# A transformer kernel's projections: products for maxima held back until their tiles have had a fixed while

## The chip, the cores and the metric

The kernel runs on one core of one Trainium2 chip. The metric is the time of one execution on the device in microseconds (us), as the median of several runs. A matrix product runs on TensorE (PE), with its weight loads listed apart (PEld); VectorE is DVE, ScalarE is ACT, GpSimd is POOL, and SyncE is SP, whose queue issues nearly all DMAs.

## The reference

Two layers, each an attention block and a feed-forward block, both with a layer norm ahead and a residual around. S = 2048 rows, D = 640, 32 heads of 20, F = 1536, all float32.

```python
x = A_x
x = x + _A_ref(_layernorm(x), A_wqkv, A_wo)
x = x + _B_ref(_layernorm(x), B_w1, B_b1, B_w2, B_b2)
x = x + _A_ref(_layernorm(x), A_wqkv, A_wo)
x = x + _B_ref(_layernorm(x), B_w1, B_b1, B_w2, B_b2)
```

_A_ref projects to q, k and v, forms scores q k^T / sqrt(20) for each head, takes the softmax over the 2048 keys, multiplies by v and projects back with wo. _B_ref is (relu(x w1 + b1))^2 w2 + b2.

## The kernel before, in words

Each layer has three stages: projections with a good part of the maxima (qkv, lines 728 to 997), attention (lines 1010 to 1222), and the output projection with the feed-forward block (add_heads and mlp). The first layer's projections fill the trace to about 310 us and the second layer's the stretch from 1757 to 2048 us.

Operands of the projections and of the scores are split into a high and a low part of a type that TensorE takes in one pass, and a product is the sum of three part products. The results q and k are therefore stored to DRAM in three parts (d_qk, and d_kd for differences of neighbouring key blocks) by SP, from a tile named ev that ScalarE and GpSimd fill, and read back into tiles of another layout (k, q, kd), in which one half of the partitions holds even heads and the other odd ones.

The softmax needs the maximum of each row of scores first. The kernel gets it by a pass of its own: products of queries by keys (by_queries, line 477), whose 512 results VectorE reduces to one number. There are two forms. A *single* (smax, line 488; "one" in the planner) is one product and one reduction (L492). A *double* (step_one and both_one, lines 535 and 543) takes two blocks of keys at once: one product with the difference of the two key blocks (tile kd), a Relu on ScalarE (L540), a second product with one of the blocks, and one sum-and-maximum on VectorE (L548). So a double spends half the VectorE time per product.

Heads go in groups g of four, queries in blocks qb of 512 rows (t = 4 g + qb), keys in blocks c of 512. A group of work in the planner is (g, qb, c), where c is 0 to 3 for singles and "d" or "e" for doubles (blocks 0 and 1, or 2 and 3). It has eight pairs (p, sub) of PAIRS, each done for par = 0 and 1.

The projection stage is written as one stream by a planner that runs while the program is built. Its units are pairs (tb, pos) of a row block and a column block (UNITS, line 724), followed by the products for v; each unit is 15 products for each half of the 128 partitions, and the two halves run side by side (product, line 310; L330 in the trace). The planner has a clock, now, that says how far it takes TensorE, VectorE and ScalarE to be: a step of two half products adds 0.235 us to now["pe"] (0.155 in the v part, line 962), a set of transposes 1.2 (line 865), and a product for maxima takes the place of one half product in a step. At each step insert() (line 854) asks whether the next bank of PSUM is free by that clock; if so, choose() (line 816) takes the next piece of work, otherwise, or if choose() gives None, the half product of the projections runs.

following() (line 796) hands out the pieces. When its queue is empty it takes the next group from its list (groups for singles, double for doubles), asks for that group's tiles with tiles() (line 771), which issues DMAs on SP only for tiles that aren't there, asks for the tiles of the next one or two groups of the list too, and fills the queue with the group's eight pairs.

Tiles are mostly asked for earlier than that, at fixed places of the stream (lines 972 to 988), by the lists PLAIN and DOUBLE (lines 705 to 718): the tiles of a single group are asked for two units before the group is entered in groups, those of the first double group two units before the doubles are entered. soon holds groups whose tiles were asked for. end_group() (line 782) gives up a q tile when no group in soon, in the lists or in the queues needs it; a tile needed later is then loaded again.

SP issues in order, and a store of ev waits there until GpSimd has filled the tile, with all requests behind it.

The projection stage ends with its last product. What is not done of the maxima by then goes to the list todo of attention (line 1024), in pairs: one entry is one (t, p, sub, c), with both halves of partitions. In attention an order written out by hand (ORDERS, line 1002) interleaves the scores, the exponentials, the products with v and the maxima of later blocks, for eight tiles of keys at a time. The number of pairs in it, 12 to 16, is chosen by pairs() (line 1183): 8 times the pairs that must be done by a block's start over the tiles left until then, collected as a debt, and at least 12. The order of 12 repeats one pattern of nine operations; the others are irregular. In the order of 12, a third of the pairs is done in halves of 256 keys (smax_half, L527). The exponentials are ScalarE's (L615, L617).

Of the kernel before, what the change touches and what calls it, by code (L numbers as in the profile page):

```python
# [39 lines left out]
def tile_layers(  # L40
# [26 lines left out]
    def slot(shape, dtype, label):  # L67
        return arena.tile(shape, dtype, tag="slot", name=name(label))
# [362 lines left out]
    def rows_of_heads(dst, src, g):  # L431
        src = src[4 * g * DH : (4 * g + 4) * DH]
        src = src.rearrange("(a b d) s t -> b (d s) a t", a=2, b=2)
        for par in range(2):
            dma(nc.sync, dst[64 * par : 64 * par + 3 * DH], src[par])

    def load_k(g, c, keep):

        if not keep:
            k = slot([P, 2, QB], F32R, "k")  # L440
        elif (g % 4, c) in kept:
            k = kept[g % 4, c]
        else:
            k = kept[g % 4, c] = slot([P, 2, QB], F32R, "k")
            for par in range(2):
                dma(nc.sync, k[64 * par + 60 : 64 * par + 62], d_one)
        k_t[g, c] = k
        rows_of_heads(k, d_qk[1, c], g)

    def load_q(t):  # L450
        g, qb = divmod(t, NQB)
        q_t[t] = slot([P, 2, QB], F32R, "q")
        rows_of_heads(q_t[t], d_qk[0, qb], g)

    def load_kd(g, x):
        k_t[g, x] = slot([P, 2, QB], F32R, "kd")
        rows_of_heads(k_t[g, x], d_kd["de".index(x)], g)
# [266 lines left out]
    UNITS = [(tb, pos) for tb in range(NQB) for pos in range(FIRST)]  # L724
    UNITS += [(tb, pos) for pos in range(FIRST, 10) for tb in range(NQB)]
    READY = 0.9

    def qkv(first, x_src, rest, scores):

# [5 lines left out]
        turning = []  # L735
        now = {"pe": 0.0, "dve": 0.0, "act": 0.0}
        busy = [0.0] * 8
        early, late, soon = {}, {}, []
        coming = [y for x in DOUBLE for h in x for y in h if y[2] == "d"]

        def at(when, n, f):
# [29 lines left out]
        def tiles(x):  # L771
            g, qb, c = x
            for c in [c] if c in range(4) else [c, 2 * "de".index(c)]:
                if (g, c) not in k_t:
                    if c in range(4):
                        load_k(g, c, g > 1)
                    else:
                        load_kd(g, c)
            if g * NQB + qb not in q_t:
                load_q(g * NQB + qb)  # L780

        def end_group(x):
            g, qb, c = x
            t = g * NQB + qb
            rest = soon + groups + double + [w[0] for w in work + twos] + [o["w"][0] for o in begun]
            if t == 0:
                left[t] -= 1 if c in range(4) else 2
            if (t or left[t]) and all(y[:2] != (g, qb) for y in rest):
                del q_t[t]
            use = {(y[0], y[2]) for y in rest + coming}  # L790
            use |= {(h, 2 * "de".index(y)) for h, y in use if y not in range(4)}
            for y in [y for y in k_t if y[0] == g and y not in use]:
                if g < 2 or y[1] not in range(4):
                    del k_t[y]

        def following(todo, queue):

            if not queue:
                if not todo:
                    return None  # L800
                x = todo.pop(0)
                tiles(x)
                for y in todo[: 2 if len(xt_) < NQB else 1]:
                    tiles(y)
                queue.extend((x, p, sub) for p, sub in PAIRS)
            return queue.pop(0)
# [9 lines left out]
        def choose():  # L816

            kind = state["last"]
            if kind == "one" or not (groups or work):
                if begun and begun[0]["ready"][0] < now["pe"] and len(begun[0]["r"]) == 2:  # L820
                    return begun.pop(0) | {"kind": "both"}
                if len(begun) < 2:
                    w = following(double, twos)
                    if w:
                        begun.append({"kind": "step", "w": w, "r": [], "ready": []})
                        return begun[-1]
            w = following(groups, work)
            return {"kind": "one", "w": w} if w else None
# [57 lines left out]
        def step_rest():  # L886
# [3 lines left out]
            if turn:  # L890
                turning.append((max(now["dve"] + READY, N * 0.235 - 0.1), turn))

# [60 lines left out]
        for j in range(len(chains)):  # L953
# [20 lines left out]
            if step % 2 == 0 and 0 <= b <= NQB:  # L974
                if b < NQB and PLAIN[b][step // 2]:
                    tiles(PLAIN[b][step // 2][0])
                    soon.append(PLAIN[b][step // 2][0])
                new = PLAIN[b][0] if step and b < NQB else PLAIN[b - 1][1] if not step and b else []
                groups.extend(new)
                soon[:] = [y for y in soon if y not in new]  # L980
                if step and b < NQB and DOUBLE[b][0]:
                    tiles(DOUBLE[b][0][0])
                    soon.append(DOUBLE[b][0][0])
# [393 lines left out]
    def layer(first, x_a, x_m, x_e, front_0, ahead):  # L1377
        xs = []
        scores = attention(first, x_a, xs)
        qkv(first, x_a, front_0, scores)  # L1380
        next(scores, None)
        steps = []
# [191 lines left out]
```

## Time and profile before

| what | value |
|---|---|
| median of 3 runs | 3500.96 us (3500.59 to 3501.50) |
| the profiled execution | 3503.38 us, its span 3501.0 us |
| PE, PEld busy | 3483.9 us (100%), 2184.4 us (62%) |
| DVE, ACT, POOL busy | 2726.4 us (78%), 2603.0 us (74%), 811.1 us (23%) |
| L492, singles' reduction | 2092, 686 ns on the mean |
| L527, reduction of two halves | 984, 682 ns |
| L548, doubles' reduction | 510, 689 ns |
| L540, doubles' Relu | 510, 597 ns |
| clock granted to TensorE, mean | 1.0 |

All times in views of the trace are microseconds from the start of the span. In a timeline, a row gives start and length, engine, line, operation, tiles and count; a bracket at its end is the time that the engine stood idle before it, with what it waited for. Matmuls overlap, and their ends are modelled, so a busy PE is not a PE at its peak; its gaps are the safer reading. In a row of the windows, the columns are the stretch, its length, then for each engine the busy time with the number of instructions in brackets, in the order PE, PEld, DVE, ACT, POOL, then the granted clock, the busy share of the DMA engines and GB/s. Where a row is for one source line alone, only its engine stands there.

### The profile page before, as it was taken

To read this page: it belongs to the slowest core of one execution; us is meant where nothing else is said; L and a number is where in the kernel's file an instruction comes from. 1 tells how busy PE (TensorE), PEld (TensorE's weight loads), DVE (VectorE), ACT (ScalarE), POOL (GpSimd) and SP (SyncE) were. 2 spreads that over 40 slices of the span, in tenths; PEclk is the share of its full clock that TensorE was granted. 3 is DMA by queue.
4 is the path that set the end of the run, shared out by engine and by line. 5 is a ranking of instruction groups with operands and counts; after the bars stand their busy time and mean duration, and the time that the engine had idled before them with its cause. 6 is when DMAs were issued, how large, how long until landed. Compare 5 with 4: busy or idle time off the path is not lost.

```text
span 3501.0 us, 69729 instructions
## 1 busy us (share of the span) xinstructions
PE 3483.9 (100%) x26544; PEld 2184.4 (62%) x26544; DVE 2726.4 (78%) x5023; ACT 2603.0 (74%) x4218; POOL 811.1 (23%) x927
## 2 busy tenths in 40 slices
PE   9999999999999999999999999999999999999999
PEld 7897444444444446999988964444444444479998
DVE  8878999999999993455567789999999999824443
ACT  3778999999999994222237789999999999932221
POOL 6530444221221121111153201211211221211110
PEclk9999999999999999999999999999999999999999
DMA  9766555323211136734477652232232111376221
GB/s 300 277 232 177 177 156 166 111 71 83 58 49 51 45 114 215 252 106 109 134 268 247 201 153 69 77 83 59 71 83 61 46 49 44 115 237 231 79 80 38
DMA packets 377404, 452.69 MB, mean 129 GB/s; under 512 B 176642, under 2 KB 223746, under 8 KB 377070
## 3 DMA queue, kind: packets, MB, share of 16 engines
q1 hardware_dynamic: 376254, 445.89, 42.1%
q8 instruction: 208, 3.41, 0.4%
q10 hardware_dynamic: 816, 2.36, 0.2%
q14 instruction: 126, 1.03, 0.1%
HBM read 273.83 MB, written 174.30 MB: 128 GB/s over the span
## 4 chain that ended last, share of the span: by engine, by line
PE 96%; DVE 1%; DMA 1%; issue 1%; ACT 0%; POOL 0%; SPq 0%; DVEq 0%
PE banks L621 29%; PE banks L480 20%; PE banks L607 14%; PE banks L292 13%; PE banks L1340 10%; PE banks L330 10%; DMA q<-d_qk 1%; PE banks L1172 0%; ACT e L1179 0%; DVE bst L243 0%; DVE mx L492 0%; SPq L76 0%; DVE xnT L256 0%; DVE x L251 0%; DMA d_qk<-ev 0%
## 5 line engine op out<-in xcount | busy, mean ns | idle before, releaser
L492 DVE TENSOR_REDUCE mx<-banks 128x1 f32<-128x512 f32 x2092 | 1427.0, 686 | 155.3 <-PE banks L480 51.3
L480 PE MATMUL banks<-k,q 60*128 60x256 f32 (+1 forms) x4570 | 1313.7, 369 | 3.5 <-DVE v L376 1.8
L480 PEld LDWEIGHTS banks<-k,q 60*128 60x128 f32 x4570 | 729.7, 184 | 880.0 <-DVE mx L527 814.3
L615 ACT ACTIVATE e<-banks 128x512 f32<-128x512 f32 x1988 | 1198.1, 608 | 23.3 <-PE banks L607 4.6
L607 PE MATMUL banks<-q,k 62*128 62x512 f32 x3968 | 1095.8, 424 | 0.7 <-DVE mx L548 0.7
L621 PE MATMUL banks<-e,vg 128*32 128x512 f32 x8192 | 1091.8, 605 | 1.5 <-ACT e L1179 1.5
L617 ACT ACTIVATE e<-banks 128x1024 f32<-128x1024 f32 x990 | 1015.3, 1026 | 0.3
L527 DVE TENSOR_REDUCE mx<-banks 128x2 f32<-128x512 f32 x984 | 671.3, 682 | 1.7 <-PE banks L480 1.7
L607 PEld LDWEIGHTS banks<-q,k 62*128 62x128 f32 x3968 | 584.3, 184 | 15.4 <-ACT e L615 6.8
L548 DVE CUSTOM_DVE_ANT_0 rl<-banks,rl 128x512 f32<-128x512 f32 x510 | 332.7, 689 | 101.2 <-PE banks L480 90.6
L330 PE MATMUL banks<-xnT,wqk 64*128 64x512 f32 x2400 | 378.5, 394 | 0.3 <-ACT mark_t L332 0.3
L1325 ACT ACTIVATE r<-banks,b_t 128x512 f32<-128x512 f32 x96 | 66.2, 690 | 419.8 <-PE banks L292 418.5
L540 ACT ACTIVATE rl<-banks 128x512 f32<-128x512 f32 x510 | 270.8, 597 | 99.3 <-PE banks L480 91.2
L1340 PE MATMUL banks<-w,h 128*128 128x320 f32 x2304 | 340.4, 309 | 0.0
L1340 PEld LDWEIGHTS banks<-w,h 128*128 128x128 f32 x2304 | 339.2, 188 | 1.3
L292 PE MATMUL banks<-xnT,w 128*128 128x512 f32 x1440 | 329.4, 389 | 0.0
L621 PEld LDWEIGHTS banks<-e,vg 128*32 128x32 f32 x8192 | 161.1, 108 | 261.8 <-issue 240.3
L330 PEld LDWEIGHTS banks<-xnT,wqk 64*128 64x128 f32 x2400 | 285.8, 185 | 34.6 <-issue 2.4
L292 PEld LDWEIGHTS banks<-xnT,w 128*128 128x128 f32 x1440 | 269.6, 188 | 55.3
L665 POOL TENSOR_TENSOR few<-few,minus_t 128x16 f32<-128x16 f32 x62 | 179.9, 2901 | 357.0 <-DMA few<-d_s 350.7
L270 POOL CAST mr<-nt 128x32 fp32r<-128x32 f32 x64 | 13.5, 211 | 943.0 <-DVE nt L574 915.0
L330 PE MATMUL banks<-wv,xnT 64*128 64x320 f32 x1920 | 199.1, 307 | 0.9 <-ACT mark_t L332 0.9
(90 smaller groups left out, 2280.7 us busy)
## 6 DMA issues: line engine op xcount, KB each, us to landing
q<-d_qk SPq DMA_DIRECT2D x242, 240.0 KB
d_qk<-ev SPq DMA_DIRECT2D x80, 512.0 KB
k<-d_qk SPq DMA_DIRECT2D x152, 240.0 KB
x<-d_x SPq DMA_DIRECT2D x84, 320.0 KB
d_qk<-ev SPq DMA_DIRECT2D x80, 256.0 KB
d_o<-ot SPq DMA_DIRECT2D x248, 80.0 KB
ot<-d_o SPq DMA_DIRECT2D x38, 512.0 KB
d_v<-v SPq DMA_DIRECT2D x32, 512.0 KB
```

Source lines behind the costliest of these rows:

```text
L292: nc.tensor.matmul(dst, a, b, start=(n == 0), stop=(n == last))
L330: m = nc.tensor.matmul(ch["dst"][:, :width], *pair, start=first, stop=last)
L480: return nc.tensor.matmul(dst, q_t[t][b : b + 60, p, sub * P : (sub + 1) * P], k_t[t // NQB, c][b : b + 60, p, keys], start=True, stop=True,)
L492: nc.vector.tensor_reduce(maxima(t)[:, 2 * par + p, sub, c : c + 1], dst, axis=AX.X, op=ALU.max)
L527: r = nc.vector.tensor_reduce(maxima(t)[:, p : p + 3 : 2, sub, c if not half else column(t, p, sub)], bank.rearrange("q (r k) -> q r k", r=2),
L540: nc.scalar.activation(res, dst, AF.Relu)
L548: nc.vector.tensor_tensor_reduce(out=r, in0=dst, in1=r, scale=1.0, scalar=LEAST, op0=ALU.add, op1=ALU.max, accum_out=maxima(t)[:, 2 * par ...
L607: nc.tensor.matmul(dst, k_t[t // NQB, kt // 4][b : b + 62, p, (kt % 4) * P : (kt % 4 + 1) * P], q_t[t][b : b + 62, p, :], start=True, stop ...
L615: nc.scalar.activation(es[h], dst, AF.Exp, scale=SCALE)
L617: nc.scalar.activation(es[pair], banks[:, 1:3, :], AF.Exp, scale=SCALE)
L621: nc.tensor.matmul(acc[32 * h : 32 * h + 32, :], v_t[t // NQB, kt // 8][:, kt % 8, 32 * h : 32 * h + 32], es[h], start=(kt == 0), stop=(kt ...
L1340: nc.tensor.matmul(dst[:, :HALF], hs[f][:, hx, i * P : (i + 1) * P], w_2.piece(at_2(f0 + f, hw, hf)), start=(f == 0 and (hx, hw) == THREE[0]),
```

## The change

following() used to take a group off its list and begin it at once. Now it asks for the group's tiles and leaves the group on the list until landed() is true: until the planner's clock for TensorE stands at least 10.7 us (singles) or 11.7 us (doubles) past the moment at which the group's key tile and its q tile were asked for, whichever was later. Until then following() returns None. In choose() a double that is held lets a single through; if there is none either, insert() returns False and the projections go on. tiles() writes down when each tile was asked for. The request for the tiles of the groups after it stays behind the start of the group, and so comes after the hold. No instruction is added, and none waits for anything new.

```diff
--- before.py
+++ after.py
@@ -724,6 +724,7 @@
     UNITS = [(tb, pos) for tb in range(NQB) for pos in range(FIRST)]
     UNITS += [(tb, pos) for pos in range(FIRST, 10) for tb in range(NQB)]
     READY = 0.9
+    LANDS = {False: 10.7, True: 11.7}
 
     def qkv(first, x_src, rest, scores):
 
@@ -735,7 +736,7 @@
         turning = []
         now = {"pe": 0.0, "dve": 0.0, "act": 0.0}
         busy = [0.0] * 8
-        early, late, soon = {}, {}, []
+        early, late, soon, asked = {}, {}, [], {}
         coming = [y for x in DOUBLE for h in x for y in h if y[2] == "d"]
 
         def at(when, n, f):
@@ -772,12 +773,19 @@
             g, qb, c = x
             for c in [c] if c in range(4) else [c, 2 * "de".index(c)]:
                 if (g, c) not in k_t:
+                    asked[g, c] = now["pe"]
                     if c in range(4):
                         load_k(g, c, g > 1)
                     else:
                         load_kd(g, c)
             if g * NQB + qb not in q_t:
+                asked[g, qb, "q"] = now["pe"]
                 load_q(g * NQB + qb)
+
+        def landed(x):
+            g, qb, c = x
+            late = c not in range(4)
+            return now["pe"] >= max(asked.get(y, -99) for y in ((g, c), (g, qb, "q"))) + LANDS[late]
 
         def end_group(x):
             g, qb, c = x
@@ -798,8 +806,11 @@
             if not queue:
                 if not todo:
                     return None
-                x = todo.pop(0)
+                x = todo[0]
                 tiles(x)
+                if not landed(x):
+                    return None
+                todo.pop(0)
                 for y in todo[: 2 if len(xt_) < NQB else 1]:
                     tiles(y)
                 queue.extend((x, p, sub) for p, sub in PAIRS)
```

## The prediction

> **What bounds the kernel now.** I read the page first, for the time and the chain of waits; then the PE timeline of the two projection stages for every gap; then the SP timeline for the requests that end in those gaps; then the busy times by stage.
>
> ```profile
> span 3501.0 us, 69729 instructions
> ...
> PE 96%; DVE 1%; DMA 1%; issue 1%; ACT 0%; POOL 0%; SPq 0%; DVEq 0%
> ```
>
> The chain that ends last is TensorE almost throughout; transfers hold 1% of it. The change touches only the two projection stages, so the question is what TensorE loses there. Gaps stand in brackets in the PE timeline: one in the first layer, four in the second.
>
> ```profile
> 74.97 0.62 PE L330 MATMUL banks<-xnT,wqk 64*128 64x512 f32 x3
> 76.72 0.47 PE L480 MATMUL banks<-kd,q 60*128 60x512 f32 x1 [1.13 <-DMA q<-d_qk]
> ...
> 1785.10 0.47 PE L480 MATMUL banks<-k,q 60*128 60x512 f32 x1 [0.31 <-DMA q<-d_qk]
> 1785.76 0.70 PE L480 MATMUL banks<-k,q 60*128 60x512 f32 x3 [0.18 <-DMA q<-d_qk]
> ...
> 1795.98 0.46 PE L480 MATMUL banks<-k,q 60*128 60x512 f32 x1 [1.18 <-DVE mx L474]
> ...
> 1816.52 0.47 PE L480 MATMUL banks<-kd,q 60*128 60x512 f32 x1 [1.83 <-DMA q<-d_qk]
> ```
>
> Each is the first product of a group: (0,1,d) at 76.72 and 1816.52, (0,0,0) at 1785.10 and 1785.76 (its two halves of rows), (1,0,0) at 1795.98. The last is put down to a memset of VectorE (L474); no product reads that, and the request of q (1,0) had gone out 5 us before, so I count it as a transfer too. Sum: 1.13 + 0.31 + 0.18 + 1.18 + 1.83 = 4.63 us.
>
> ```profile
> 69.50 7.08 DMA q<-d_qk
> ...
> 1779.54 0.85 SPq L76 DMA_DIRECT2D q<-d_qk  x2
> ...
> 1790.96 0.82 SPq L76 DMA_DIRECT2D q<-d_qk  x2
> ...
> 1799.22 0.95 SPq L76 DMA_DIRECT2D q<-d_qk  x2
> ...
> 1805.33 0.99 SPq L76 DMA_DIRECT2D kd<-d_kd  x2
> ...
> 1807.33 9.06 DMA q<-d_qk
> ...
> 1778.00:1785.00 7.00, 6.80 (x60) 5.27 (x58) 0.00 (x0) 2.44 (x8) 3.67 (x3) 1.00 0.97 305
> ...
> 1796.00:1816.00 20.00, 18.69 (x156) 17.84 (x156) 18.42 (x30) 4.58 (x12) 6.41 (x6) 1.00 1.02 324
> 1816.00:1850.00 34.00, 33.48 (x280) 27.94 (x282) 27.98 (x71) 19.09 (x41) 17.90 (x19) 1.00 0.98 348
> 1850.00:1900.00 50.00, 50.00 (x422) 40.36 (x420) 39.34 (x124) 38.47 (x80) 19.07 (x20) 1.00 0.63 225
> ```
>
> The first rows are requests and landings of q (SP timeline and chain), the last four the stages of the second layer (PE, PEld, DVE, ACT, POOL, clock, DMA share, GB/s). While the gaps occur the 16 DMA engines are full (0.97 to 1.02), and q takes 7 to 9 us from issue to landing; from 1850 on there is room (0.63) and TensorE has no gap.
>
> **The change part by part.** It adds no instruction. It reorders TensorE's stream: a group's products stay out until the planner's clock stands 10.7 (11.7 for d and e) past the request, and projection matmuls run in their place, as insert() returns False.
>
> Which groups are held follows from the planner's arithmetic. Requests go out two units ahead: 2 x 15 steps x 0.235 = 7.05, plus 1.2 for each set of transposes between, plus 0.1175 for each product inserted. For (0,0,0) that is 10.65 in the first layer (three sets) and 7.05 in the second. In the second layer (1,0,0) follows with 7.05 + 16 x 0.1175 = 8.93, then (0,0,1) with 9.63 and (0,1,d) with 9.40; in the first layer (0,1,d) has 8.93, and the others have 11.5 or more. Later groups are requested when the group ahead begins, so they have the length of a group.
>
> ```profile
> 30.00:308.00 278.00, 164.37 (x501) 1.00 0.78 260
> ...
> 1785.61 9.71 DVE mx L492 x16
> ```
>
> The first row counts L548: two records each, so 250 reductions of doubles between 76.7 and 308, 0.93 us apart, 16 in a group: 14.8 us, more than 11.7 (by the planner's clock at the least 11.87). So these aren't held, or by a step. The second row is the first single group: 16 reductions in 9.71 us by the trace, 8.93 by the planner.
>
> Held are then: first layer, (0,0,0) by one step and (0,1,d) by 11.7 - 8.93 = 2.77 us; second layer, (0,0,0) by 3.65 and (0,1,d) by 1 to 2.3. (1,0,0) now starts at the end of the delayed (0,0,0), 12.6 after its request, and (0,0,1) about 13.5 after its own.
>
> *Stalls.* At (0,0,0), 3.65 later than 1785.1 is past both landings: 0.49 gone. (1,0,0) comes at about 1757.5 (first projection matmul of the layer) + 40.85 = 1798.3, past 1795.98: 1.18 gone. First layer, (0,1,d): 2.77 exceeds 1.13, and the five or so single products that run in between have their tiles: 1.13 gone.
>
> (0,1,d) in the second layer is the tight one. Nine products fewer lie before its request, which comes at 45.2 instead of 46.1; it is released at 56.9, on the trace 1814.4. Its q landed at 1807.33 + 9.06 = 1816.4, on full engines, so an earlier request alone doesn't bring it sooner. But (0,0,0) now ends (40.85) after line 977 has entered (0,0,1) in soon, so end_group keeps q (0,0), which before was deleted and loaded again at 1799.22.
>
> ```profile
> q<-d_qk SPq DMA_DIRECT2D x242, 240.0 KB
> ```
>
> That takes 2 x 240 KB off the queue, at 324 to 348 GB/s 1.4 us: landing about 1814.9, left over 0.5 us. Bounds: 0, when the landing moves along with the 2.6 us by which TensorE is earlier, and 2.0, when the reload gives nothing. I take 0.5, as it comes from the rate of the very window. The Trainium skill (DMA: Bandwidth & Descriptors, Specifications) gives a fabric ceiling of 435 GB/s; the fullest window here shows 348. By the page's figure the remaining queue would be gone before 1814.4, an estimate that makes the left-over zero; the measured rate decides.
>
> *Moved requests.* following() asks for the next group's tiles only after the hold: for (1,1,d), four issues of SP, 1.3 to 2.8 us later than before, past a few stores of ev. Their products begin 23 us after that; nothing.
>
> *Products that slip.* What isn't done in the projections is done in attention. Second layer: 3.65 us without singles is 6.5 products; 1.3 come back as the pause of 0.7 us before (0,0,1) goes, and about one as singles and doubles then run together. Some 4.2 are missing when doubles begin, 5.5 at the end, since projections are two steps further on: 1.4 sets of a double's four products. First layer: about 1.9 products, 0.4 sets. In the projections each is worth 50.00 / 422 = 0.118 us of TensorE (row of 1850): 7.4 x 0.118 = 0.87 us saved.
>
> In attention each set comes back as two of the pairs in todo.
>
> ```profile
> 308.00:1352.00 1044.00, 675.00 (x984) 1.00 0.36 102
> ...
> 308.00:1352.00 1044.00, 335.65 (x492) 1.00 0.36 102
> ...
> 2047.00:3092.00 1045.00, 672.34 (x980) 1.00 0.27 74
> ...
> 2047.00:3092.00 1045.00, 335.67 (x492) 1.00 0.27 74
> ...
> 517.84 1.00 PE banks L621 x8
> ...
> 519.85 1.00 PE banks L621 x8
> ...
> 1317.08 1.00 PE banks L621 x8
> ...
> 1319.09 0.99 PE banks L621 x8
> ...
> 900.00:932.60 32.60, 32.60 (x259) 14.53 (x257) 30.52 (x51) 32.33 (x51) 6.62 (x7) 1.00 0.20 52
> ```
>
> Reductions L492 and L527 in attention, by layer: (984 + 492) / 2 = 738 pairs, and 736. pairs() divides by 496 - 3 - 1 = 492 tiles: 8 x 738 / 492 = 12.00. The first layer sits exactly on the smallest pace; the second has two pairs to spare. Each pair beyond makes one order of 12 an order of 13. The trace shows none. Below: with products (517.84) and without (1317.08) a tile of attention takes 2.01 us, as ScalarE is full (32.33 of 32.60), so a pair may cost nothing; a gain has no way in, as the count of activations stays. Above: two reductions end to end, 2 x 0.69 = 1.4 us. By VectorE's share, 30.52 of 32.60 a block or 15.26 of 16.3 an order, 26 / 24 of that is 16.5: 0.2 us. I take that, as it is the row of the same stage. Sets are whole: layer one slips 0 or 1, layer two 1 or 2, so 0 to 4 such orders; I take 2: 0.4 us.
>
> *Sum*, against the profiled execution of 3503.38 us (span 3501.0): -4.63 + 0.5 - 0.87 + 0.4 = -4.6, so 3498.8. That execution lies 2.42 above the median of 3500.96; on the median's level: 3496.4 us, 0.13% less. About 0.2%, 7 us, is what I treat as the least that a measurement of this kernel can tell from no change.
>
> **The rivals.** *The queue sets the pace (stalls stay).* TensorE reaches (0,1,d) and (1,0,0) earlier, stores of ev come earlier, and full engines (1.02) deliver no sooner; holds only trade places with stalls. For it: the share of DMA in 1778 to 1850. Against: the hold exceeds the stall at four of five gaps. It gives 0.49 + 0.87 - 0.4 = 1.0 less, and up to 2 with the first layer's gap: 3499.5. The Trainium skill (DMA: Bandwidth & Descriptors, Queues, rings and completion order) says that an engine consumes descriptors in ring order; by that rule a load waits for all stores asked before it, which is this rival; the landings of 7 to 9 us in the rows agree with it, though none shows the order itself.
>
> *The slipped maxima cost more than the stalls.* Place: attention, orders of 13, which leave the regular alternation of the order of 12. Price: up to 1.4 us each. If two sets slip in the first layer (4 pairs) and three in the second (6, two of them free), there are 8: 11.2 us, against 4.1 + 20 x 0.118 = 6.5 saved: 4.7 slower, 3505.7. It decides from four orders at 1.4 us, or 27 at 0.2. For it: 12.00 exactly, and VectorE at 94%. Against: ScalarE is the fuller, and my count is 0 to 4.
>
> *A larger gain.* If holds recur in later groups by steps and 25 products more slip into free attention, 4.1 + 32 x 0.118 = 7.9 less: 3493.1. Against: 14.8 us per group.
>
> *It does nothing.* The clock that counts is the planner's; if it ran ahead of TensorE holds would end too early. But the request at 1779.54 and the product at 1785.10 lie as the planner has them (7.05 apart from the first issue at 1778.05). It gives 3501.
>
> **How the numbers follow.** Forecast 0.60, queue 0.14, slipped maxima 0.14, larger gain 0.08, nothing 0.04. Only the larger gain passes 7 us downwards, and only the worst third of the slipped maxima, plus a point for what I don't see, upwards: faster 0.08, same 0.86, slower 0.06. Low: all stalls gone, twice the slip, orders free, -4.63 - 1.75 = -6.4, and part of the larger gain: 3493.0. High: past the queue's and the idle case to part of the slipped maxima: 3503.0.
>
> **What would show it.** Right: no bracketed gap at these five places; first layer-two product at about 1789; two q issues fewer in the second layer's projections; L492 plus L527 in attention up by 0 to 4 pairs a layer; attention's blocks at 32.6 us. Wrong: a gap above 1 us before a kd product; attention longer by more than 2 us; more than 6 pairs slipped in a layer.

## The result and the profile after

The changed kernel takes 3549.27 us (median, 3548.64 to 3551.31) beside 3500.78 for the kernel before: a ratio of 1.0141, 95% interval 1.0129 to 1.0153. The forecast was 3496.4 in a range of 3493.0 to 3503.0. It is wrong, in sign too. From the page of the profile after: its length, the chain by engine, and the loads of q.

```profile
span 3549.5 us, 69631 instructions
...
PE 95%; ACT 2%; DVE 1%; issue 1%; POOL 0%; DMA 0%; ACTq 0%; POOLq 0%; DVEq 0%
...
q<-d_qk SPq DMA_DIRECT2D x240, 240.0 KB
```

The share of transfers in the chain is gone, and two loads of q as well; but ScalarE, at 0% before, now holds 2%. The PE timeline after, at the groups that had waited (first (0,1,d) of the first layer; (0,0,0) and (0,1,d) of the second):

```profile
77.75 0.39 PE L480 MATMUL banks<-kd,q 60*128 60x512 f32 x1
...
1809.16 0.63 PE L480 MATMUL banks<-k,q 60*128 60x512 f32 x4
...
1834.95 0.39 PE L480 MATMUL banks<-kd,q 60*128 60x512 f32 x1
```

No bracket is left at any of the five places, and no gap over 0.2 us has come up at another product for maxima while the projections run. So the holds do what they say. Where the time went shows when the two traces are cut into stages. First the chain: where the first layer's attention ends (L292, before and after), where the second layer's projections begin (L330), and where its attention ends (L292). Before:

```profile
1353.70 2.39 PE banks L292 x15
...
1757.47 3.64 PE banks L330 x29
...
3094.06 2.39 PE banks L292 x15
```

After:

```profile
1374.60 2.39 PE banks L292 x15
...
1778.37 3.64 PE banks L330 x29
...
3141.99 2.40 PE banks L292 x15
```

20.9 us are lost by the first of these marks, and 27.0 more between the second and the third. The wide exponentials of ScalarE (L617, one for each tile of keys, 495 a layer in the ordinary orders) part projections from attention: their first and last starts, before

```profile
L617 ACT ACTIVATE e<-banks x495: 1015/1017/1107, 313.7 to 1321.0; 128x1024 f32<-128x1024 f32 x165
...
L617 ACT ACTIVATE e<-banks x495: 1016/1017/1107, 2053.2 to 3061.4; 128x1024 f32<-128x1024 f32 x165
```

and after:

```profile
L617 ACT ACTIVATE e<-banks x495: 1015/1018/1113, 315.6 to 1341.9; 128x1024 f32<-128x1024 f32 x165
...
L617 ACT ACTIVATE e<-banks x495: 1017/1018/1114, 2066.5 to 3109.3; 128x1024 f32<-128x1024 f32 x165
```

The stretch from first to last is attention: 1007.3 and 1008.2 before, 1026.3 and 1042.8 after, 53.6 us more in the two layers. The projections of the second layer are 7.6 shorter (2066.5 - 1778.37 = 288.1 against 295.7), those of the first 1.9 longer. So the loss lies in attention, which the change does not touch; only the number of pairs left to it differs (VectorE's reductions after, L492 and then L527, first layer and second):

```profile
308.00:1374.00 1066.00, 686.44 (x1004) 1.00 0.35 100
...
308.00:1374.00 1066.00, 324.82 (x476) 1.00 0.35 100
...
2062.00:3140.00 1078.00, 697.47 (x1024) 1.00 0.26 72
...
2062.00:3140.00 1078.00, 313.91 (x460) 1.00 0.26 72
```

(1004 + 476) / 2 = 740 and (1024 + 460) / 2 = 742 pairs, against 738 and 736. Six pairs are more than the smallest pace carries, and pairs() gives two orders of 13 in the first layer and four in the second; L527, which only the order of 12 has, falls by 48, eight for each. Six orders out of some 124. Counting wide exponentials eight by eight finds them at once: in the kernel before nearly every stretch takes 16.1 to 16.6 us, here the six take 24.6, 25.3, 23.3, 23.2, 24.4 and 26.1, and a stretch right beside one up to 17.1. The first, in the windows of L617 alone, with the stretch before it:

```profile
691.30:707.60 16.30, 7.64 (x8) 1.00 0.10 28
707.60:732.20 24.60, 8.24 (x8) 0.93 0.55 147
```

Eight exponentials in both, 24.6 us instead of 16.3. All engines over an ordinary order of the kernel before, and over that stretch:

```profile
700.00:716.30 16.30, 16.30 (x128) 7.27 (x128) 15.28 (x27) 16.13 (x26) 1.54 (x3) 1.00 0.40 97
...
707.60:732.20 24.60, 20.04 (x124) 7.15 (x116) 16.63 (x29) 15.78 (x24) 6.58 (x7) 0.93 0.55 147
```

ScalarE works 15.8 us of it, no more than before, and VectorE 16.6, 1.35 more for its two further reductions; neither comes near 24.6. TensorE's gaps over the stretch are put down to the exponentials:

```profile
L607 PE MATMUL banks<-q,k 62*128 62x512 f32 x32 | 10.8, 466 | 4.6 <-ACT e L617 4.2 <-ACT e L615 0.2
```

That is 4.6 us of standing still before scores (L607), 4.2 of them for a wide exponential; an ordinary order has none. Two excerpts show how, the PE timeline and the ACT timeline:

```profile
708.81 0.50 PE L607 MATMUL banks<-q,k 62*128 62x512 f32 x1 [0.23 <-ACT e L617]
708.82 0.50 PE L480 MATMUL banks<-k,q 60*128 60x512 f32 x1
709.15 0.65 PE L607 MATMUL banks<-q,k 62*128 62x512 f32 x3
709.39 0.65 PE L480 MATMUL banks<-k,q 60*128 60x512 f32 x2
711.21 0.50 PE L607 MATMUL banks<-q,k 62*128 62x512 f32 x1 [1.17 <-ACT e L617]
```

```profile
710.14 1.02 ACT L617 ACTIVATE e<-banks 128x1024 f32<-128x1024 f32 x1
711.04 0.61 ACT L615 ACTIVATE e<-banks 128x512 f32<-128x512 f32 x1
713.23 1.02 ACT L617 ACTIVATE e<-banks 128x1024 f32<-128x1024 f32 x1 [1.58 <-PE banks L480]
```

At 711.21 a score waits 1.17 us until the wide exponential has read its bank; all that stands behind it on TensorE waits too, among it the scores for which ScalarE then idles 1.58 us. (The ACT view names L480, a product for maxima; an exponential reads scores alone, and the last of them, L607, runs beside it.)

### The profile page after: what moved, and what is told of

It reads as the page before. It is cut to its first block, busy times and chain, and to the rows that moved or that the text cites. A ratio compares the mean times of both kernels' runs of the same rounds, so it can differ in the third digit from the quotient of the medians.

```text
span 3549.5 us, 69631 instructions
## 1 busy us (share of the span) xinstructions
PE 3510.6 (99%) x26498; PEld 2180.5 (61%) x26498; DVE 2733.6 (77%) x5023; ACT 2600.3 (73%) x4212; POOL 809.2 (23%) x928
## 3 DMA queue, kind: packets, MB, share of 16 engines
q8 instruction: 208, 3.41, 0.4%
## 4 chain that ended last, share of the span: by engine, by line
PE 95%; ACT 2%; DVE 1%; issue 1%; POOL 0%; DMA 0%; ACTq 0%; POOLq 0%; DVEq 0%
PE banks L621 28%; PE banks L480 20%; PE banks L607 14%; PE banks L292 13%; PE banks L330 10%; PE banks L1351 10%; ACT e L617 1%; ACT e L615 1%; PE banks L1183 0%; ACT e L1190 0%; DVE mx L492 0%; DVE bst L243 0%; DVE xnT L256 0%; DVE x L251 0%; PE banks L407 0%
## 5 line engine op out<-in xcount | busy, mean ns | idle before, releaser
L492 DVE TENSOR_REDUCE mx<-banks 128x1 f32<-128x512 f32 x2156 | 1463.1, 686 | 198.6 <-PE banks L480 88.6
L480 PE MATMUL banks<-k,q 60*128 60x512 f32 (+1 forms) x4530 | 1317.7, 373 | 3.0 <-DVE v L376 1.8
L480 PEld LDWEIGHTS banks<-k,q 60*128 60x128 f32 x4530 | 723.1, 185 | 865.3 <-DVE mx L527 768.0
L607 PE MATMUL banks<-q,k 62*128 62x512 f32 x3968 | 1109.0, 427 | 25.8 <-ACT e L617 24.0
L617 ACT ACTIVATE e<-banks 128x1024 f32<-128x1024 f32 x990 | 1016.5, 1027 | 15.6 <-PE banks L480 12.5
L527 DVE TENSOR_REDUCE mx<-banks 128x2 f32<-128x512 f32 x936 | 638.7, 682 | 0.0
L607 PEld LDWEIGHTS banks<-q,k 62*128 62x128 f32 x3968 | 585.9, 185 | 78.8 <-ACT e L617 46.8
L330 PE MATMUL banks<-xnT,wqk 64*128 64x512 f32 x2400 | 377.4, 394 | 0.3 <-ACT mark_t L332 0.3
L540 ACT ACTIVATE rl<-banks 128x512 f32<-128x512 f32 x504 | 268.2, 598 | 101.8 <-PE banks L480 97.1
L292 PE MATMUL banks<-xnT,w 128*128 128x512 f32 x1440 | 329.4, 390 | 0.0
L330 PEld LDWEIGHTS banks<-xnT,wqk 64*128 64x128 f32 x2400 | 283.2, 186 | 37.5 <-issue 2.4
L292 PEld LDWEIGHTS banks<-xnT,w 128*128 128x128 f32 x1440 | 269.8, 188 | 55.1
L330 PE MATMUL banks<-wv,xnT 64*128 64x320 f32 x1920 | 199.0, 308 | 1.3 <-ACT mark_t L332 1.3
```

Source lines behind the costliest of these rows:

```text
L292: nc.tensor.matmul(dst, a, b, start=(n == 0), stop=(n == last))
L330: m = nc.tensor.matmul(ch["dst"][:, :width], *pair, start=first, stop=last)
L480: return nc.tensor.matmul(dst, q_t[t][b : b + 60, p, sub * P : (sub + 1) * P], k_t[t // NQB, c][b : b + 60, p, keys], start=True, stop=True,)
L492: nc.vector.tensor_reduce(maxima(t)[:, 2 * par + p, sub, c : c + 1], dst, axis=AX.X, op=ALU.max)
L527: r = nc.vector.tensor_reduce(maxima(t)[:, p : p + 3 : 2, sub, c if not half else column(t, p, sub)], bank.rearrange("q (r k) -> q r k", r=2),
L540: nc.scalar.activation(res, dst, AF.Relu)
```

## The experiments

Three theories stood at the start. P: an order of 13 costs some 8.5 us through its irregular sequence. Q: through its thirteenth pair. H: these orders stand there by chance, and holding back the maxima spoils attention in another way. In all texts below the six places are those that the changed kernel has; the cost of an order is the growth of the L617 stretch, both layers, over 1007.3 + 1008.2 = 2015.5 us, divided by six.

**Orders of 13 alone.** The kernel before, with pairs() cut to

```
state["calls"] = state.get("calls", -1) + 1
return 13 if state["calls"] in ((24, 47) if first else (13, 27, 40, 54)) else 12
```

> The kernel before, with nothing held in the projections, but with six orders of 12 in attention replaced by the order of 13 at the places where the changed kernel has them (calls 24 and 47 of the first layer, 13, 27, 40 and 54 of the second). If the orders of 13 cost the time (theory P, by their irregular sequence, and theory Q, by the thirteenth pair itself): 6 x 8.5 us = 51 us more than before, about 3552 us. If the holds in the projections cost it by another way and these orders stand there by chance (theory H): 3501 us.

Measured 3550.37 us (ratio 1.0149, 1.0133 to 1.0164).

```profile
L617 ACT ACTIVATE e<-banks x495: 1016/1018/1112, 312.2 to 1335.6; 128x1024 f32<-128x1024 f32 x165
...
L617 ACT ACTIVATE e<-banks x495: 1016/1018/1112, 2065.5 to 3108.7; 128x1024 f32<-128x1024 f32 x165
```

1023.4 and 1043.2: 51.1 us more, 8.5 an order, with nothing held and not one pair more to do. H falls.

**The order of 13 in the usual pattern.** The changed kernel, with

```diff
-        13: "baanmbVmbanambbnbmVanbmnaVnaabnmbVanbmaanVnmbbanaVmnbmabVabbmmnaVm",
+        13: "mbmbananV" * 2 + "ubmbawnaV" * 6,
```

> The changed kernel, with the order of 13 written in the pattern of the order of 12: two tiles with two whole pairs each, then six tiles of the usual nine operations. Scores come in the usual sequence b, b, a, a. Theory P: the holds are left alone with their gain in the projections, 5.7 us by the two traces, and six orders cost at most 1 us each: 3495 to 3501 us. Theory Q (thirteen pairs are more than VectorE or TensorE carries in that time): still 8 us an order, 3545 us. Theory H: 3549 us.

Measured 3504.22 us (1.0011, 1.0001 to 1.0020). The stretches are 1009.9 and 1012.3: 6.7 us, 1.1 an order. Q falls: thirteen pairs fit. The total lies 3 us above what was expected: six even orders cost 6.7 us and not at most 6, and the projections gain less than the two traces had it (below).

**Twelve pairs in the irregular sequence.** As the first run, with one m and one n taken out near the end of that order.

> As the run with six orders of 13 in the kernel before, but with one pair taken out of the order of 13, so that it holds 12 pairs in the irregular sequence of scores. Theory P: nearly the same cost as with 13, 6 x 7 to 8.5 us, 3543 to 3552 us. Theory Q: no cost, 3501 us. Theory H: 3501 us.

Measured 3551.73 us (1.0147, 1.0132 to 1.0162), 8.5 an order. The thirteenth pair adds nothing to the irregular order. P stands, if its "sequence" is taken for the whole order of the operations.

**Doubles held, singles not.** `LANDS = {False: 0.0, True: 11.7}`

> The changed kernel with doubles held (11.7 us) and singles not. By the planner's arithmetic the first layer leaves 740 pairs to attention, as with the whole change, and the second 736, as before: two orders of 13 instead of six. Theories P and Q: the first layer as with the whole change (21 us longer than before), the second shorter by its stall of 1.83 us: about 3520 us. Theory H, if the holds of doubles do it: 3549 us; if those of singles: 3500 us.

Measured 3516.2 us (1.0047, 1.0032 to 1.0062), 4 below the 3520 expected: two orders of 13 and a first-layer stretch of 1024.2, 16.9 more than before: 8.5 an order again. The cost follows the number of such orders, 0, 2 and 6.

What in the irregular order costs? It differs in two ways: the *sequence* in which scores of the two halves (a, b) come, and the *places* of maxima and products with v between them. The places include that it has no maxima in halves (u and w), which the order of 12 has.

**Its places, the usual sequence.** The changed kernel, order 13 with its scores renamed b, b, a, a throughout: `"bbanmaVmbbnamabnbmVanamnbVnbaanmbVbnamabnVnmbaanbVmnbmaaVbbammnaVm"`

> The changed kernel, with the order of 13 as it is but for the names of its 32 scores: at the same places they come b, b, a, a throughout, as in the order of 12. Products for maxima and products with v stay where they were. If the sequence of the scores is the cause (theory P1: with b, a, a, b the wide exponential of heads 0 and 3 waits for the fourth score, and the next tile's score for the bank that it reads): an order costs 1 to 2 us as the even one does, 3504 to 3511 us. If the uneven places of the products with v and of the maxima are the cause (theory P2): 8 us an order, 3545 to 3550 us.

Measured 3514.82 us (1.0039, 1.0025 to 1.0052); 16.1 us of attention, 2.7 an order, at thirteen pairs.

**Each tile's scores turned, all else usual.** The kernel before, six times `"ubmaawnbV" * 8` in place of the order of 12.

> The kernel before, with the usual order of 12 at the six places but for its scores, which come b, a, a, b in each tile. Everything else is as in the usual order. Theory P1: 5 to 8 us an order, 3530 to 3552 us. Theory P2: no cost, 3500 us.

Measured 3518.81 us (1.0051, 1.0036 to 1.0067); 2.9 an order by the stretches (1013.5 and 1019.5; the text of the next run has 2.3 for it). Neither P1 nor P2 holds in its pure form: both runs lie between the two expectations.

**Its sequence, the usual places.** The kernel before, six times the order of 12 with the 32 letters of order 13: `"ubmaawnbVubmaawnbVubmbawnbVuamaawnbVubmabwnaVuambbwnaVuambawnbVuambbwnaV"`

> The kernel before, with six orders of 12 whose operations stand at the usual places (u, score, m, score, score, w, n, score, V in each tile), but whose 32 scores come in the sequence of the order of 13: b a a b b a a b b b a b a a a b b a b a a b b a a b a b a b b a. Together with the run that had the order of 13's places and the usual sequence (2.65 us an order) and the one with b, a, a, b in each tile (2.3 us), it tells which part of the 8.3 us is left. If the sequence with its runs of three scores on one half is the cause: 7 to 8 us an order, 3543 to 3550 us. If sequence and places must come together: 2 to 4 us an order, 3513 to 3525 us, and TensorE's clock stays at 1.0 in these orders.

Measured 3523.92 us (1.0067, 1.0053 to 1.0081); 3.7 an order, clock at 1.0.

**Its places, the usual sequence, twelve pairs.** The kernel before, six times `"bbanmaVmbbnamabnbmVanamnbVnbaanmbVbnamabnVnmbaanbVmnbmaaVbbamaVm"`

> The kernel before, with six orders that have the places of the order of 13 (one pair taken out, 12 left) and the usual sequence of scores b, b, a, a. It closes the table of sequence and places at 12 pairs: the sequence alone cost 3.7 us an order, both together 8.5. If the parts add up but for TensorE's clock: places alone 1.6 to 2 us an order, 3510 to 3513 us, clock 1.0 in these orders. If the places alone carry the missing part: 4.8 us an order, 3529 us.

Measured 3515.33 us (1.0049, 1.0032 to 1.0066); 2.4 an order, clock at 1.0.

At twelve pairs, an order costs: sequence 3.7, places 2.4, both 8.5. They don't add up: 2.4 us an order are left. The traces show where. TensorE's wait before scores over the second layer's attention, with its four such orders: both, the sequence alone, the places alone.

```profile
L607 PE MATMUL banks<-q,k 62*128 62x512 f32 x1977 | 554.5, 427 | 16.7 <-ACT e L617 15.3 <-ACT e L615 0.8
...
L607 PE MATMUL banks<-q,k 62*128 62x512 f32 x1977 | 552.4, 425 | 2.4 <-ACT e L617 1.1 <-ACT e L615 0.9
...
L607 PE MATMUL banks<-q,k 62*128 62x512 f32 x1977 | 549.3, 425 | 1.2 <-ACT e L617 1.2
```

An order stands still 4.2 us with both, but 0.6 and 0.3 with one of them (0.0 in the kernel before): 3.3 more than the parts together. So the long wait for a wide exponential needs both, and it is enough to hold the 2.4. TensorE's clock, too, is halved in these orders only where both come together. The granted clock in the run with both, the stretch ahead of one such window and the window:

```profile
2988.80:2992.20 3.40, 2.21 (x15) 1.01 (x15) 2.03 (x4) 2.00 (x3) 3.17 (x3) 0.99 0.36 107
2992.20:2995.60 3.40, 3.40 (x18) 1.03 (x14) 1.15 (x2) 0.67 (x2) 0.00 (x0) 0.50 0.37 96
```

That run has five such windows of 3.4 us in its six orders, in which at most half of 17 us is lost: up to 1.4 us an order, an estimate. How much of the 2.4 is the clock's and how much the wait's stays open.

**Holds that need no order of 13.** Holding in the second layer alone, singles by 8.3 us:

```diff
+            if first:
+                return True
-    LANDS = {False: 10.7, True: 11.7}
+    LANDS = {False: 8.3, True: 11.7}
```

> The changed kernel, holding in the second layer alone, singles 8.3 us and doubles 11.7. By the planner's arithmetic 738 pairs are left in both layers, so that no order of 13 is needed. If the stalls are worth what the gaps show (0.49 + 1.83, and most of 1.18, plus 0.5 for four products fewer): 3.5 us less than before, 3496.5 us, with first exponential of the second layer 291 to 292 us after the layer's first projection (before: 293.6 to 295.8). If what is saved in the projections is lost elsewhere: 3500 us.

Measured 3496.9 us (0.9989, 0.9980 to 0.9998): 4.0 less than the 3500.94 before of the same chip. The gain of the holds is there once their price in attention is not. The second layer's projections have no gap left, and its first exponential comes 289.8 us after their start, a little earlier than expected; the pairs are 738 in both layers.

**Singles held, doubles not, even order of 13.** `LANDS = {False: 10.7, True: 0.0}`, order 13 as in the second run.

> The changed kernel with singles held and doubles not, and the even order of 13. By the planner's arithmetic 738 and 742 pairs. First layer: one step of one hold is all that differs from before. If the 2.5 us that the changed kernel's first projections take more come of the doubles' hold, the first exponential is at 312 to 314 us; if of that one step, at 315 to 316. Second layer: (0,0,0) and (1,0,0) held, the stall of 1.83 us at (0,1,d) stays: 290 us to the first exponential; attention 4 us longer for four even orders. Time 3500 us.

Measured 3500.96 us (0.9999, 0.9990 to 1.0008). The first wide exponential comes at 310.8: the one step is no loss. With doubles held alone it came at 313.2, with both at 315.6 to 315.9 in three profiles, and in eight profiles of the unchanged first layer at 312.2 to 313.7. Only the two holds together delay it, as far as one or two profiles of each part can tell. The stall of 1.83 us at (0,1,d) did not just stay, it grew:

```profile
1810.98 0.47 PE L480 MATMUL banks<-kd,q 60*128 60x512 f32 x1 [2.83 <-DMA q<-d_qk]
```

TensorE had lost nothing at the groups ahead and came there 4.2 us sooner after the layer's first projection than before (53.1 against 57.2), the tile of q only 3.1 sooner.

**Light holds in both layers.** First layer: singles 10.7, doubles none; second: 8.3 and 11.7.

> The changed kernel with the holds that leave 738 pairs in both layers: in the first layer singles alone, 10.7 us (one step of one group), in the second singles 8.3 and doubles 11.7. No order of 13 is used. If the gains seen in single runs add up (first exponential of the first layer at 310.8 instead of 312.2 to 313.7, the second layer's projections at 289.8 instead of 293.6 to 295.8): 5 to 7 us less than before, 3495 us. If the first layer's 310.8 was scatter: 3497 us.

Measured 3495.74 us (0.9987, 0.9978 to 0.9996), 4.7 less than before and between the two expectations; the first layer's 311.4 is too near 312.2 to be called a gain. The stretches of L617:

```profile
L617 ACT ACTIVATE e<-banks x495: 1015/1017/1132, 311.4 to 1319.3; 128x1024 f32<-128x1024 f32 x165
...
L617 ACT ACTIVATE e<-banks x495: 1015/1017/1130, 2045.6 to 3053.7; 128x1024 f32<-128x1024 f32 x165
```

Attention is back at 1007.9 and 1008.1. This version has the lowest median of all; beside the second-layer one the difference is within the scatter.

**No second load of q (0,0).** The kernel before, with `if x != (0, 0, 0) and ...` ahead of the condition in end_group().

> The kernel before, with nothing held, but keeping the q tile of (0,0) after the first group, so that it isn't loaded a second time in the second layer (480 KB less on the queue). If the reload is a part of the stall at (0,1,d), the gap there falls from 1.83 us (1.5 to 2.2 in the runs so far) to about 0.4, and the time by 1.4 us to 3499.5. If the landing is set by something else, the gap stays at 1.5 to 2.2 and the time at 3501.

Measured 3498.7 us (0.9996, 0.9987 to 1.0005). Its profile has no gap at (0,1,d) in the second layer, but one of 0.91 at (1,0,0). That does not show the reload to be the cause. Of six profiles with the reload and nothing held in that layer, four show 0.37 to 2.18 at (0,1,d) and two (the orders of 13 alone, the irregular twelve) none, but 1.87 and 1.97 at (1,0,0). The run with singles held alone has no reload either (240 requests of q), and it has the largest gap of all there, 2.83. So the gap comes without the reload and stays away with it; what sets the landing is open.

## Why the prediction was wrong

*The stalls.* Right that all five gaps go; the left-over of 0.5 at (0,1,d) did not show. The size, 4.63, came from a single execution. In six profiles of the same projections, before's among them, the gaps at these places sum to 2.3 to 4.6, and before's is the highest. The sum took the whole 4.63 and then 2.42 more because that execution lay above the median, so a part may have been counted twice; no run shows how much.

*The reload.* Right that it falls away (240 requests of q instead of 242). That this is what closes the gap is not borne out: without the reload, but with doubles not held, the gap was 2.83.

*The projections as a whole.* 4.63 - 0.5 + 0.87 = 5.0 less was the working. Beside the one profile of before they came out 7.6 - 1.9 = 5.7 shorter. That the two are so near is luck. Over the six profiles the second layer's projections took 293.5 to 295.7 us to the first exponential, against 288.1, so its gain is 5.4 to 7.6; and the first layer lost 1.9 to 3.7 us, which the working did not have. Its doubles then wait more for the Relu on ScalarE: from 100 to 200 us the weight loads of L480 idle 8.2 to 8.3 us for L540 in the three profiles with both holds, and 3.2 to 5.0 in the eleven others. Why the two holds together bring that about stays open.

*The slip.* Too small. The working had 1.4 sets of a double in the second layer and 0.4 in the first; it was three and one. It counted the products missing when doubles begin at the pace of singles, and took what the pause gave back as kept; by the planner's clock the last group (2,0,e) then begins 3.5 us later and the stage ends 1.5 earlier, 5.0 us at some 2.4 products each: 12 products. "0 to 4 such orders; I take 2" should have been six, outside its own bounds. Alone that would have been a small error: at 0.2 us an order, six are 1.2 us.

*The price of an order.* This is the step that failed: "Above: two reductions end to end, 2 x 0.69 = 1.4 us. By VectorE's share ... 0.2 us. I take that". Measured 8.5 to 8.9. With six orders that is 51 to 54 us, the whole loss. The bound priced the pair that is added. But an order of 13 puts all of its 32 scores, 26 maxima and 8 products with v in other places, and attention has no room for that: in an ordinary block ScalarE is busy 32.33 of 32.60 us and TensorE has no gap. The working priced the engines' work and put the waits between TensorE and ScalarE at nothing; in the first of these orders TensorE alone stands still 4.6 us. The text even said that the orders of 13 "leave the regular alternation", and then priced that at 1.4 us. A pair in an even order costs 1.1 us, near the bound; it is the order written for it that costs 8.

*The rivals.* The one on the other side had the place and the mechanism and, at a chance of 0.14, the wrong size: its 3505.7 counted eight orders at 1.4. With the measured price it decides from the first order, since 4.1 + 0.118 x 4 = 4.6 saved is less than 8.5. The queue rival ("stalls stay") is refuted for the change as a whole, as no gap is left. But its mechanism shows where doubles are not held: TensorE comes 4.2 us sooner, the tile 3.1, and the gap at (0,1,d) is 2.83.

*What was to show it right* did so in part: gaps, requests, and pairs up by 2 in the first layer; in the second they rose by 6, not 0 to 4. "More than 2 us longer attention" was named as the sign of the error, and is it.

## What to carry to other kernels

Work that is moved out of a stage lands in another, and there it isn't priced by its own instructions but by what it does to the order that the other stage runs in; a planner that sits exactly on a threshold (12.00 here) makes that a step, not a slope. Before pricing such a step by engine shares, read the two sequences side by side: with a bank that one engine reads late and a stream on the other that waits as a whole, the same twelve pairs in another sequence and other places took half of an order's time again. And tune a hold by what it removes in the stage and by whether it still leaves the next stage on the near side of its threshold: in the second layer 8.3 us for singles instead of 10.7 did both, but for a gap of 0.39 in one of two profiles.

## What the runs showed of the hardware

TensorE's clock was halved without TensorE having stood still for long. In the changed kernel, the stretch ahead and the window:

```profile
720.30:723.70 3.40, 2.21 (x19) 1.01 (x15) 2.15 (x4) 2.00 (x3) 0.00 (x0) 1.00 0.37 94
723.70:727.10 3.40, 3.40 (x18) 1.03 (x14) 0.95 (x2) 0.46 (x1) 2.88 (x3) 0.50 0.43 128
```

TensorE was busy 2.21 of 3.4 us, its longest gap 1.19 us, and for the next 3.4 us the granted clock was 0.50. The Trainium skill (TensorE: Matmul & The Clock Gate, Why this matters for your kernels) warns of idle gaps above about 3 us; shorter ones were enough here. By the clock records of all runs the clock was halved 20 times between a program's start and its end, and in the 3.41 us ahead TensorE was busy 1.77 to 2.54 us, with a longest gap of 0.9 to 2.0. What decides it isn't shown. In the same trace a stretch that is as busy, with a gap as long (1.19 us), was followed by the full clock:

```profile
2529.40:2532.80 3.40, 2.21 (x16) 0.83 (x15) 1.46 (x4) 1.77 (x3) 0.00 (x0) 1.00 0.00 0
2532.80:2536.20 3.40, 2.48 (x23) 0.85 (x19) 2.13 (x4) 2.53 (x5) 0.00 (x0) 1.00 0.01 2
```

The kernel before has the halving once as well, where attention of the second layer begins:

```profile
2048.60:2052.00 3.40, 1.76 (x17) 1.06 (x16) 1.80 (x8) 2.17 (x4) 0.00 (x0) 1.00 0.00 0
2052.00:2055.40 3.40, 3.40 (x16) 1.33 (x16) 2.22 (x5) 2.11 (x3) 0.21 (x1) 0.50 0.38 154
```

In the run with six irregular orders of 12 and in the one with doubles held alone it also came once in the second layer's projections, at 1814, after gaps of 1.97 and 1.54 us in which a group's first product waited for q. So a short wait for a transfer can cost more than its bracket shows.
